# Three score tiles to one exp, half-length DFTs and a planned order of matmuls in an attention-plus-spectral-filter kernel

## The chip, the cores and the metric

The kernel runs on one core of a Trainium2 chip. The metric is the device time of one execution in microseconds. A run is called fast or slow here as the records label it: slow is a run more than 1.5% above the fastest of the same kernel. Times are medians of all runs of a session with the range beside them; ratios are of fast runs only: the mean time of one kernel's fast runs over the mean of the other's fast runs of the same rounds, so not quite the ratio of the medians that are quoted. Engines in the profile: PE is TensorE's matmuls, PEld its weight loads, DVE is VectorE, ACT is ScalarE, POOL is GpSimd, SP the queue that issues most transfers.

## The reference, cut to what matters

```python
def reference(A_x, A_wqkv, A_wo, B_x, B_w_r, B_w_i):     # S = 2048, D = 448, H = 16, Dh = 28, bf16
    # A: full softmax attention
    q, k, v = split(A_x @ A_wqkv)
    p = softmax(einsum("bhqd,bhkd->bhqk", q, k) * Dh ** -0.5)
    a = einsum("bhqk,bhkd->bhqd", p, v).reshape(B, S, D) @ A_wo
    # B: a filter in the frequency domain
    X = rfft2(B_x.astype(float32)) * (B_w_r + 1j * B_w_i)
    b = irfft2(X, s=(S, D)).astype(bfloat16)
    return concatenate([a, b], axis=-1)                  # ... (cut)
```

The exp of 16 x 2048 x 2048 scores is ScalarE's. With four heads side by side in 32-row strips of TensorE (the kernel's `tile_position`; four such score matmuls take 0.33 us until the next group starts, in the trace of the kernel before), there are 1024 score tiles of 128x512. Everything else (projections, both DFTs, output projection) has to find room on the other engines beside those exps.

## The kernel before

An exp takes two score tiles (1024 columns). The scores of four tiles are issued ahead of it, the value matmuls and one step of other work behind it, and two matmuls of zeros per round:

```python
while n < NU:                                   # NU = 512 pairs of tiles
    for m in pair: emit_act(m)                  # ACTIVATE Exp, 128x1024
    for m in reversed(pair): emit_st(m + NST)   # score matmuls, 28 rows of a 32-row strip each
    for m in pair: emit_pv(m)                   # value matmuls, 32 columns each
    ...                                         # (cut) one step of a projection or of the DFT
    if kc_l < KC - 1:
        emit_dummy(dbg.get("dummies", 2))       # matmuls of zeros, 128x128x512, into the accumulator
```

The softmax sums are brought to a 128x16 tile before the reciprocal:

```python
for t in range(4):
    ins = e.matmul(zv[:, 4*t:4*t+4], oaug[:, g, 128*t:128*(t+1)], identb[:, 128:132], start=True, stop=True)
...
e.reciprocal(rzT[:, g, :], zv)                  # 128x16
...                                             # (cut) spread by one copy and 16 small matmuls
```

The DFT of length 2048 is done as 128 x 16, with twiddle products on VectorE and 16-row matmuls on TensorE.

The softmax here doesn't subtract the row's maximum and nothing guards it: scores larger than these inputs give would overflow.

Of the kernel before, what the change touches and what calls it, by code (L numbers as in the profile page):

```python
# [12 lines left out]
_ENG = ("sp", "act", "pe", "dve", "pool")  # L13


class Prog:

    def __init__(self, nc, sems):
        self.nc = nc
        self.streams = {e: [] for e in _ENG}  # L20
        self.sems = sems
        self.count = {name: 0 for name in sems}
        self.wm = {e: {name: 0 for name in sems} for e in _ENG}
        self.trk = {}
        self.consts = set()
        self.csem = {"sp": "dma_sp", "act": "act", "pe": "pe", "dve": "dve", "pool": "pool"}
        self.ninstr = {e: 0 for e in _ENG}
        self.dma_sems = set(n for n in sems if n.startswith("dma") or n.startswith("out"))
# [8 lines left out]
    def _need_waits(self, eng, reads, writes):  # L37
# [14 lines left out]
        for k in reads:  # L52
            en = self._entry(k)
            add(en["w"])
# [5 lines left out]
        return waits  # L60

    def _emit_waits(self, eng, waits):
        for s, v in sorted(waits.items()):
            semh = self.sems[s]
            self.streams[eng].append(lambda e, semh=semh, v=v: e.wait_ge(semh, v))
            self.wm[eng][s] = v
            self.ninstr[eng] += 1

    def op(self, eng, fn, reads=(), writes=(), sem=None, inc=1, signal=True):
        waits = self._need_waits(eng, reads, writes)  # L70
        self._emit_waits(eng, waits)
        if sem is None:
            sem = self.csem[eng]
        if signal:
            self.count[sem] += inc
            ev = (sem, self.count[sem])
            semh = self.sems[sem]
            self.streams[eng].append(lambda e, fn=fn, semh=semh, inc=inc: fn(e).then_inc(semh, inc))
        else:
            ev = None  # L80
            self.streams[eng].append(lambda e, fn=fn: fn(e))
        self.ninstr[eng] += 1
        for k in reads:
            if k in self.consts:
                continue
            en = self._entry(k)
            if ev is not None:
                en["r"].append(ev)
        for k in writes:
            en = self._entry(k)  # L90
            if ev is not None:
                en["w"] = ev
                en["r"] = []
        return ev

    def dma(self, eng, fn, reads=(), writes=(), sem=None):
        if sem is None:
            sem = {"sp": "dma_sp", "pool": "dma_pool", "act": "dma_act"}[eng]
        assert sem in self.dma_sems
        return self.op(eng, fn, reads=reads, writes=writes, sem=sem, inc=16)  # L100
# [19 lines left out]
def _lowprec(nc, msg, thunk):  # L120
    with nc.allow_low_precision(msg):
        return thunk()




def partb_constants():
    S, D = 2048, 448
    KD = 225
    NQ = 4  # L130
    NBQ = [15, 14, 14, 14]
    KD0 = [0, 60, 116, 172]
    d = np.arange(D)
    kd = np.arange(KD)
    CD = np.zeros((128, 4, 450), np.float64)
    ang = 2 * np.pi * np.outer(np.arange(D), kd) / D
    full = np.concatenate([np.cos(ang), -np.sin(ang)], axis=1)
    full[:, 225] = 0.0
    full[:, 225 + 224] = 0.0
    for c in range(3):  # L140
        CD[:, c, :] = full[128 * c:128 * c + 128, :]
    CD[64:128, 3, :] = full[384:448, :]
    s1 = np.arange(128)
    th = 2 * np.pi * np.outer(s1, s1) / 128
    F128 = np.stack([np.cos(th), np.sin(th), -np.sin(th)], axis=1)
    k2 = np.arange(16)
    s2 = np.arange(16)
    W16 = np.exp(-2j * np.pi * np.outer(k2, s2) / 16)
    Cw = W16.real
    Sw = -W16.imag  # L150
    G16 = np.exp(2j * np.pi * np.outer(s2, k2) / 16)
    Gc = G16.real
    Gs = G16.imag
    mats = [Cw.T, Sw.T, -Sw.T, Gc.T, Gs.T, -Gs.T]
    W16C = np.zeros((128, 6, 32), np.float64)
    for i, m in enumerate(mats):
        for r in range(4):
            W16C[32 * r:32 * r + 16, i, 0:16] = m
    th2 = 2 * np.pi * np.outer(np.arange(128), np.arange(16)) / 2048
    TW = np.zeros((128, 16, 4), np.float32)  # L160
    TW[:, :, 0] = np.cos(th2)
    TW[:, :, 1] = -np.sin(th2)
    TW[:, :, 2] = np.sin(th2)
    cfac = np.full(KD, 2.0)
    cfac[0] = 1.0
    cfac[224] = 1.0
    ang2 = 2 * np.pi * np.outer(kd, d) / D
    CRe = cfac[:, None] * np.cos(ang2) / (S * D)
    CIm = -cfac[:, None] * np.sin(ang2) / (S * D)
    CDinv = np.zeros((128, 4, 448), np.float64)  # L170
    quarters = []
    for q in range(NQ):
        k0 = KD0[q]
        nk = 4 * NBQ[q]
        re_hi = min(k0 + nk, 225)
        nre = re_hi - k0
        im_lo = max(k0, 1)
        im_hi = min(k0 + nk, 224)
        nim = im_hi - im_lo
        CDinv[0:nre, q, :] = CRe[k0:re_hi, :]  # L180
        CDinv[64:64 + nim, q, :] = CIm[im_lo:im_hi, :]
        quarters.append(dict(q=q, k0=k0, nb=NBQ[q], nk=nk, nre=nre, nim=nim, imkk0=im_lo - k0))
    return dict(CD=CD, F128=F128, W16C=W16C, TW=TW, CDinv=CDinv, quarters=quarters)

def build_kernel(nc, A_x, A_wqkv, A_wo, B_x, B_w_r, B_w_i, out, do_a=True, do_b=True, defer=24, dbg=None):
    dbg = dbg or {}
    S = 2048
    D = 448
    DH = 28
    NG = 4  # L190
    KC = 16
    QC = 4
    RE = 4
    NST = 3
    scale = float(DH) ** -0.5

    sem_names = ["pe", "act", "dve", "pool", "dma_sp", "dma_pool", "dma_act", "dma_xa", "dma_xb", "dma_bw", "dma_wqk", "dma_wv", "dma_wo", "dma_cst", "out0", "out1", "out2"]
    ctx = ExitStack()
    with ctx:
        sems = {n: ctx.enter_context(nc.semaphore("s_" + n)) for n in sem_names}  # L200
        P = Prog(nc, sems)

        bf16np = mybir.dt.np(BF16)
        cst_np = np.zeros((128, 256), dtype=np.float32)
        cst_np[:, 0:128] = np.eye(128, dtype=np.float32)
        for j in range(4):
            cst_np[32 * j, 128 + j] = 1.0
        cst_h = nc.inline_tensor(cst_np.astype(bf16np), name="cst_bf16")
# [3 lines left out]
        xAT = sb("xAT", [128, 4, S])  # L212
        wq = sb("wq", [128, 4, NG, 128])
        wk = sb("wk", [128, 4, NG, 128])
        wv = sb("wv", [128, 4, 512])
        wo = sb("wo", [128, NG, 448])
        qT = sb("qT", [128, NG, S])
        kT = sb("kT", [128, NG, S])
        Vaug = sb("Vaug", [128, KC, 512])
        ET = sb("ET", [128, RE, 1024])  # L220
        oaug = sb("oaug", [128, NG, 512])
        onrm = sb("onrm", [128, NG, 512])
        rzT = sb("rzT", [128, NG, 16])
        rzrep = sb("rzrep", [128, 4, 128])
        identb = sb("identb", [128, 256])
        zmm = sb("zmm", [128, 512])
        astg = sb("astg", [128, 3, 448])
        bzero = sb("bzero", [128, 448]) if not (do_a and do_b) else None

        PS_all = ctx.enter_context(nc.psum_tensor("PS_all", [128, 4096], F32))  # L230
        ST_ps = PS_all[:, 0:NST * 1024]
        ACC_ps = PS_all[:, 3072:3584]
        MISC_ps = PS_all[:, 3584:4096]

        xa = A_x[0]
        col0 = [0, 128, 256, 320]
        for c in range(4):
            P.dma("sp", lambda e, c=c: e.dma_start_transpose(xAT[:, c, :], xa[:, col0[c]:col0[c] + 128]),  # L238
                  writes=[("xAT", c)], sem="dma_xa")
            P.consts.add(("xAT", c))  # L240

        WQK = [("wq", c) for c in range(4)]
        WKK = [("wk", c) for c in range(4)]
        WVK = [("wv", c) for c in range(4)]
        WOK = [("wo", g, j) for g in range(NG) for j in range(4)]
        P.op("dve", lambda e: e.memset(wq[:], 0.0), writes=WQK)
        P.op("dve", lambda e: e.memset(wk[:], 0.0), writes=WKK)
        P.op("pool", lambda e: e.memset(wv[:], 0.0), writes=WVK)
        P.op("pool", lambda e: e.memset(wo[:], 0.0), writes=WOK)
        P.op("pool", lambda e: e.memset(zmm[:], 0.0), writes=["zmm"])  # L250
        P.dma("pool", lambda e: e.dma_start(identb[:, :], cst_h.ap()[:, :]), writes=["identb"], sem="dma_cst")

        wrows = [(0, 128, 0), (0, 128, 128), (0, 128, 256), (64, 128, 384)]
        wst_holder = []

        def setup_weights():
# [734 lines left out]
```

## Time and profile before

| what | value | how to read it |
|---|---|---|
| time | 695.67 us (694.11 to 696.61, 3 runs) | |
| span of the profiled run | 691.8 us | all shares of the page are of this |
| first exp, end of the last | 28.0, about 663.4 us | 28 us before and 28 us after the exps |
| ScalarE busy with exps | 482.5 us | 153 us of idle time between them |
| zeros on TensorE | 480 matmuls, 164.7 us busy | work that computes nothing |

One more line of the page of the kernel before: the clock that was granted to TensorE in 40 slices of the span, in tenths of full speed.

```profile
PEclk9879999996999996889989967897985889965659
```

It is at full speed for most of the run, with half-clock slices near the end.

### The profile page before, as it was taken

What the parts mean: (1) busy time and instruction counts of PE and PEld (TensorE: products, weight loads), DVE (VectorE), ACT (ScalarE), POOL (GpSimd) and SP (SyncE); (2) the same over time, 40 slices, a digit from 0 to 9 for tenths busy, and PEclk for the clock granted to TensorE, in tenths of its full rate; (3) what the DMA queues carried; (4) which work ended last, traced back from release to release, by engine and by line L of the source; (5) the groups of instructions that cost most, each with busy time, mean ns of one, the idle gap of its engine ahead of it and who ended that gap; (6) DMA issues with size and microseconds to landing.
All of it is one profiled execution on the core that took longest, in us unless ns stands there. A gap on an engine that the chain in (4) does not pass through costs nothing.

```text
span 691.8 us, 11149 instructions
## 1 busy us (share of the span) xinstructions
PE 548.5 (79%) x4614; PEld 173.3 (25%) x4614; DVE 356.2 (51%) x718; ACT 483.8 (70%) x513; POOL 48.3 (7%) x38
## 2 busy tenths in 40 slices
PE   0598899967997975688797685997858868989677
PEld 0122233322321222222122222321222223212223
DVE  1323333375336368853735659336484473542856
ACT  0156698974997984679988755997874769976510
POOL 7710000000030000003000000120000000000000
PEclk9879999996999996889989967897985889965659
DMA  9900000000000200000000200000000200000003
GB/s 226 204 1 0 1 1 1 1 1 0 2 1 8 48 1 1 1 1 1 1 1 21 34 1 1 1 1 1 1 1 1 54 1 1 1 1 1 1 7 127
DMA packets 39138, 13.17 MB, mean 19 GB/s; under 512 B 34112, under 2 KB 38464, under 8 KB 39088
## 3 DMA queue, kind: packets, MB, share of 16 engines
q1 hardware_dynamic: 38272, 10.92, 7.2%
q0 software_dynamic: 816, 1.55, 0.7%
q8 instruction: 36, 0.59, 0.3%
q14 instruction: 14, 0.11, 0.1%
HBM read 4.60 MB, written 3.67 MB: 12 GB/s over the span
## 4 chain that ended last, share of the span: by engine, by line
PE 42%; DVE 31%; ACT 12%; issue 9%; DMA 3%; SPq 2%; POOL 1%; DVEq 0%; ACTq 0%; POOLq 0%
ACT ET L810 12%; PE PS_all L846 9%; PE PS_all L798 7%; PE PS_all L831 6%; PE PS_all L342 5%; DVE BT L690 5%; DVE Y1T L736 3%; PE PS_all L538 3%; DVE Y1T L733 3%; DVE Atr L596 2%; PE PS_all L359 2%; PE PS_all L642 2%; PE PS_all L470 2%; DVE Atr L595 2%; SPq L238 1%
## 5 line engine op out<-in xcount | busy, mean ns | idle before, releaser
L810 ACT ACTIVATE ET<-PS_all 128x1024 bf16<-128x1024 f32 x512 | 482.5, 1070 | 178.8 <-PE PS_all L798 175.6
L846 PE MATMUL PS_all<-zmm 128*128 128x512 bf16 x480 | 164.7, 429 | 0.0
L798 PE MATMUL PS_all<-qT,kT 28*128 28x512 bf16 x1024 | 112.1, 427 | 24.7 <-ACT ET L810 18.5
L831 PE MATMUL PS_all<-ET,Vaug 128*32 128x512 bf16 x1024 | 112.8, 430 | 0.0
L798 PEld LDWEIGHTS PS_all<-qT,kT 28*128 28x128 bf16 x1024 | 26.3, 92 | 155.5 <-ACT ET L810 112.7
L831 PEld LDWEIGHTS PS_all<-ET,Vaug 128*32 128x32 bf16 x1024 | 26.6, 94 | 72.6 <-issue 71.3
L342 PE MATMUL PS_all<-xAT,wq 128*128 128x512 bf16 x64 | 22.7, 461 | 27.2 <-DVE wq L268 18.8
L846 PEld LDWEIGHTS PS_all<-zmm 128*128 128x128 bf16 x480 | 31.8, 101 | 49.1 <-issue 45.3
L690 DVE COPY BT<-PS_all 128x512 bf16<-128x512 bf16 (+2 forms) x16 | 35.0, 2186 | 15.2 <-PE PS_all L687 15.2
L555 POOL MEMSET Atr<- 128x3840 bf16 x4 | 13.2, 3303 | 397.7 <-PE PS_all L614 397.7
L647 DVE CAST AT<-PS_all 128x512 bf16<-128x512 f32 (+2 forms) x32 | 20.2, 632 | 39.9 <-PE PS_all L642 39.9
L647 DVE CAST Xq<-PS_all 128x512 bf16<-128x512 f32 (+2 forms) x32 | 20.3, 633 | 35.8 <-PE PS_all L642 35.8
L726 PE MATMUL PS_all<-F128sb,BT 128*56 128x128 bf16 (+2 forms) x64 | 13.7, 290 | 23.7 <-DVE Y1T L736 17.0
L642 PE MATMUL PS_all<-Xq,W16sb 16*32 16x512 bf16 (+2 forms) x256 | 22.4, 426 | 4.9 <-DVE AT L647 4.9
L733 DVE CAST Y1T<-PS_all 56x128 bf16<-56x128 f32 (+2 forms) x64 | 18.0, 282 | 15.0 <-PE PS_all L729 13.4
L348 DVE CAST qT<-PS_all 128x512 bf16<-128x512 f32 x16 | 11.1, 692 | 27.2 <-PE PS_all L342 27.2
L541 DVE CAST X<-PS_all 128x450 bf16<-128x450 f32 x16 | 10.0, 627 | 29.2 <-PE PS_all L538 29.2
L538 PE MATMUL PS_all<-CD,xBT 128*128 128x450 bf16 x64 | 19.6, 408 | 6.7 <-DMA CDinv<-cst_cdinv 6.0
L348 DVE CAST kT<-PS_all 128x512 bf16<-128x512 f32 x16 | 11.1, 692 | 26.3 <-PE PS_all L342 26.3
L363 DVE CAST Vaug<-PS_all 128x512 bf16<-128x512 f32 x16 | 11.1, 692 | 23.6 <-PE PS_all L359 23.6
L342 PE MATMUL PS_all<-xAT,wk 128*128 128x512 bf16 x64 | 20.0, 413 | 3.2 <-DVE AstF L577 1.9
L470 PE MATMUL PS_all<-wo,onrm 128*128 128x448 bf16 x64 | 18.0, 423 | 5.6 <-DVE AstF L577 2.6
(90 smaller groups left out, 601.7 us busy)
## 6 DMA issues: line engine op xcount, KB each, us to landing
out_dram<-astg SPq DMA_DIRECT2D x32, 112.0 KB, 1.7
Y1T<-in_A_wqkv_dram SPq DMA_DIRECT2D x3, 336.0 KB, 4.3
CD<-cst_cd POOLq DMA_DIRECT2D x1, 450.0 KB, 4.2
CDinv<-cst_cdinv POOLq DMA_DIRECT2D x1, 448.0 KB, 4.4
Wsb<-in_B_w_r_dram SPq DMA_DIRECT2D x2, 224.0 KB, 4.0
Wsb<-in_B_w_i_dram SPq DMA_DIRECT2D x2, 224.0 KB, 3.4
wo<-in_A_wo_dram POOLq DMA_DIRECT2D x16, 24.5 KB, 4.0
Wsb<-in_B_w_r_dram SPq DMA_DIRECT2D x1, 240.0 KB, 4.1
```

The lines of the kernel that those rows point to most:

```text
L342: ins = e.matmul(mv, wsb[rlo:rhi, c, g, :], xAT[rlo:rhi, c, 512 * n:512 * (n + 1)], start=(c == 0), stop=(c == 3))
L348: P.op("dve", lambda e: e.tensor_copy(dst[:, g, 512 * n:512 * (n + 1)], mv), reads=[mkey], writes=[key])
L470: ins = e.matmul(mv, onrm[:, g, 128 * tl:128 * (tl + 1)], wo[:, g, :], start=(g == 0), stop=(g == NG - 1))
L538: ins = e.matmul(mv, xBT[rlo:rhi, c, s2::16], CD[rlo:rhi, c, :], start=(c == 0), stop=(c == 3))
L642: ins = e.matmul(o, W16sb[32 * r:32 * r + 16, wi, :], rhs, start=(term == 0), stop=(term == 1), tile_position=(32 * r, 32 * r))
L647: P.op("dve", lambda e, pout=pout, b=b, nbg=nbg: e.tensor_copy(dst[:, pout, b:b + nbg, :], MISC_ps[:, 0:nbg * 128].rearrange("p (b k) -> p ...
L690: P.op("dve", lambda e, pp=pp, b0=b0, nbat=nbat: e.tensor_copy(BT[:, pp, :, 4 * b0:4 * b0 + 4 * nbat].rearrange("p s k -> p k s"), MISC_bf ...
L733: P.op("dve", lambda e, si=si, s2b=s2b: e.tensor_copy(Y1T[0:nre, q, s2b, :], MISC_ps[0:nre, si * 128:si * 128 + 128]), reads=["MISC"], wri ...
L798: ins = e.matmul(stv[:, jj * 512:(jj + 1) * 512], kT[32 * j:32 * j + KH, g, 128 * kc:128 * (kc + 1)], qT[32 * j:32 * j + KH, g, 512 * qc:5 ...
L810: P.op("act", lambda e: e.activation(ET[:, etslot, :], stv, ACT.Exp, scale=scale), reads=[("ST", stslot)], writes=[("ET", etslot)])
L831: ins = e.matmul(ACC_ps[32 * j:32 * (j + 1), :], Vaug[:, kc, 32 * h:32 * (h + 1)], ET[:, etslot, jj * 512:(jj + 1) * 512], start=False, st ...
L846: ins = e.matmul(ACC_ps, zmm[:, 0:128], zmm[:, 0:512], start=False, stop=False)
```

## The change

The intent: three tiles to one exp (fewer instructions; exps in a row start 0.919 us apart at 1024 elements), a DFT that halves its length once and then multiplies directly by cosine and sine matrices (no twiddles, dense matmuls), and an order of matmuls planned by a list scheduler that knows a cost for each instruction. The zeros are gone. The diff is a new kernel; its core, cut:

```diff
-            P.op("act", lambda e: e.activation(ET[:, etslot, :], stv, ACT.Exp, scale=scale), ...)   # 128x1024
+    TU = 3
+            P.op("act", lambda e: e.activation(ET[:, t % NE, 0:n], PS[:, b0:b0 + n], ACT.Exp, scale=scale),
+                 reads=[("ST", t % 2)], writes=[("ET", t % NE)], cost=0.833e-3 * n + 0.08)          # 128x1536
-                    emit_dummy(dbg.get("dummies", 2))
+        KEEP = 0
-                P.op("dve", ... e.reciprocal(rzT[:, g, :], zv) ...)                                 # 128x16
+                P.op("dve", lambda e: e.reciprocal(rs[:, i, :], MISC), reads=["MISC"], writes=[("rs", i)], cost=0.68)
+                                                                                                    # 128x512
+            if cur[0] is not None and now + mm_cost(cur[0].kreads) <= st_at + 0.35:
+                step_job()            # one matmul of other work, if the plan says that it fits before the next scores
+                continue
... (cut: DFT stages as dense matmuls, complex products on GpSimd, weights loaded on ScalarE's queue)
```

`MISC` is the one PSUM bank that all other work shares: projections, DFT stages, softmax sums and output projections go through it one after the other. Six banks hold scores, one the value accumulator.

## The prediction

> **What bounds the kernel now.** I read the page's busy shares first, then the groups of instructions, then busy time by stretch, then the timeline. The page's first part and the two lines that matter of its groups:
>
> ```profile
> PE 548.5 (79%) x4614; PEld 173.3 (25%) x4614; DVE 356.2 (51%) x718; ACT 483.8 (70%) x513; POOL 48.3 (7%) x38
> ...
> L810 ACT ACTIVATE ET<-PS_all 128x1024 bf16<-128x1024 f32 x512 | 482.5, 1070 | 178.8 <-PE PS_all L798 175.6
> L846 PE MATMUL PS_all<-zmm 128*128 128x512 bf16 x480 | 164.7, 429 | 0.0
> ```
>
> No engine is saturated. The exp on ACT is the one large piece that nothing can avoid: 482.5 us busy, and 175.6 us of its idle time ended with a score matmul (L798). The tile's own listing puts the first exp at 28.0 us and the last at 662.4, about 663.4 with its own length. So the span of 691.8 is 28 us of prologue, 635 us with exps (482.5 busy, about 153 idle) and 28 us of tail. The first two are what a new kernel can win.
>
> Why are the scores late? Busy time by stretch (span; PE, PEld, DVE, ACT, POOL busy with counts; granted clock; DMA) shows two regimes:
>
> ```profile
> 190.25:207.54 17.29, 15.81 (x181) 4.18 (x177) 6.68 (x11) 17.29 (x20) 5.91 (x2) 1.00 0.00 1
> ...
> 259.43:276.72 17.29, 10.24 (x95) 3.89 (x95) 14.30 (x40) 8.36 (x9) 0.00 (x0) 0.61 0.00 1
> ...
> 622.62:639.92 17.30, 16.35 (x107) 3.83 (x106) 5.17 (x6) 11.76 (x13) 0.00 (x0) 0.57 0.00 1
> ```
>
> In the first, the clock is full and ACT is never idle. In the second, VectorE is the busy one (twiddle products and the strided copy L690, 2.43 us at its largest); the in-order PE stands behind the single MISC bank and the scores stand behind it. In the third, PE is busy but at half clock and needs about 3 us for a round of two exps. So the present bound changes: the DFT's VectorE chain, then a PE slowed by its clock, then ACT.
>
> The pace of ACT alone comes from the timeline (start, length, engine, group):
>
> ```profile
> 191.71 16.65 ACT L810 ACTIVATE ET<-PS_all 128x1024 bf16<-128x1024 f32 x18
> ...
> 305.38 0.39 PE L798 MATMUL PS_all<-qT,kT 28*128 28x512 bf16 x4
> ...
> 305.71 0.40 PE L831 MATMUL PS_all<-ET,Vaug 128*32 128x512 bf16 x4
> ...
> 306.50 0.59 PE L846 MATMUL PS_all<-zmm 128*128 128x512 bf16 x2
> ```
>
> Eighteen exps in 16.65 us, the last one 1.03 long: (16.65 - 1.03)/17 = 0.919 us from start to start. Four score matmuls in different row strips take 0.33 us until the next group starts, four value matmuls as well.
>
> [...] 617 to 634 us is solid PE work at 0.50, with much of it in 16-row matmuls. [...] The trace: RECIPROCAL of 16 elements takes 258 ns, where casts out of PSUM of 450 and 512 elements (627 and 692 ns) extrapolate to about 175 ns for 16. [...]
>
> **The change part by part.**
>
> Exp: 512 of 1024 elements become 341 of 1536 and one of 512. [...] 341 x 1.346 + 0.5 = 459 us, against 512 x 0.919 = 471. The larger instruction is worth only 12 us; the gain must come from the 153 us of idle.
>
> PE: the 480 dummies go, also the 16-row DFTs, twiddle transposes and packing transposes. From the order of the new program I counted 1024 score matmuls in 342 groups, 256 groups of four value matmuls, and 328 bursts of other work holding 388,640 columns. Cost at full clock: groups 342 x 0.33 = 113 and 256 x 0.33 = 84; [...] Sum 395 us, or 1.155 us per exp of 1.346. PE is 86% used and no longer the bound, if it stays warm; cold it would need about twice that, 2.1 us per exp. Nearly all new DFT matmuls use 112 to 128 rows and columns, so I expect warm stretches without dummies.
>
> VectorE: about 130 evacuations of 0.63 to 0.69 us, some 90 us, come in place of 356. The complex products go to POOL: eight sets of seven instructions of 512 elements[...]. In the program order they have over 100 exps (130 us) before the last is needed: hidden.
>
> The one addition I distrust is RECIPROCAL. Before it ran on 128x16; now on 128x512, sixteen times, reading the only MISC bank. If the surplus over a cast is per element, (258 - 158)/16 = 6.2 ns, so 158 + 512 x 6.2 = 3.3 us[...]. The scheduler that fixed the order gave it 0.68. Until it ends no other matmul group may use the bank, and the PE queue is in order. In 12 of the 15 cases before the tail just one score group comes between this step and the next MISC user. From the normalizing matmul at t: reciprocal ends near t+3.75, PE goes on at t+3.9, does some 0.5 us of the burst and 0.45 of scores, so ACT gets work at t+4.85. ACT has work left for two exps, 2.69 us, from an end of exp at about t+0.4: idle 1.75 us. Three cases have two score groups and lose about 0.4. Sum 12 x 1.75 + 3 x 0.4 = 22 us.
>
> The 2.9 us holes also make some clock windows fall: in the 3.4 us stretches of the kernel before, stretches with less than about 1.8 us of PE time are mostly followed by 0.50. If 60% of 15 holes do that and each costs one window and a half at 2.1 instead of 1.346 us per exp, about 1.7 us, that is 15 us.
>
> Prologue: only one input is transposed on the way in, and the weights load through the ACT queue beside it. Before, weights landed at 17.7 us after the queue's transposes; I put the first scores at 22.5 and the first exp at 23 (was 28). PE starts cold: 4 us. Five places where the order has a whole projection squeezed in ahead of the scores: 5 us.
>
> Tail, from the last exp: values and evacuation 1.4, normalizing matmul 0.6, reciprocal 3.3, product 0.8, four output groups in one bank at cold clock (1.5 matmul + 1.0 evacuation and waits each) 10, last store 2.2, waits 0.6: 19 us (was 28).
>
> Sum: 23 + 459 + 22 + 15 + 9 + 19 = 547 us of span; measured time was 3.9 above the span, so 551. I take a little less, 542, since the reciprocal may be quick (then 22 and 15 vanish and 2.5 of the tail: about 512).
>
> **The rivals.** (a) The reciprocal is cheap[...]: 512. One small sample speaks for neither[...]. (b) The clock falls without dummies: at a third of the exps cold, 114 x 0.8 = 90 us more, about 620. For it: value and score groups alone fill only 0.58 of 1.346 us. Against: the order spreads other work over nearly all exps (0.45 to 0.6 us each, 0.25 in the weight-transposing stage), which is 70 to 90% busy. (c) POOL is slower than assumed or waits on VectorE[...]. (d) DMA: about 8 MB of constants and inputs before the DFT; at the 226 GB/s of the first slice it takes 40 us, and the transforms come later in the order. Hidden.
>
> **Range and chances.** Low end: fast reciprocal, 512 plus a little, 515. High end: [...]more cold stretches, 575. Even rival (b) is far below 682, so faster is near sure: 0.98, with 0.01 for each other outcome.
>
> **What would show it.** Right: ACT busy near 460 us, exps 1.34 us start to start in runs; RECIPROCAL at 3 to 4.5 us with the following PE matmul waiting for it, and ACT idle of 1 to 2 us sixteen times; clock at 1.00 in most slices with dips near those; first exp near 23; tail near 19. Wrong: RECIPROCAL under 1 us; clock at 0.5 over long stretches; PE waiting on POOL or DMA; ACT idle spread evenly over all exps, which would mean that PE, not ACT, sets the pace.

The pace of 1.346 us, and with it the 459, was an estimate; measured afterwards it is right (0.919 us for 1024 elements and 1.346 for 1536 make 0.834 ns per element and 65 ns fixed). TensorE's 395 us were 113 + 84 + 162 for columns + 36 for changes of shape. (In e7, below, 14 matmuls of zeros occupy TensorE for 3.12 us at full clock, 2.3 columns per ns, by which the 388,640 columns take 169 us.) That the products are hidden was an assumption, and a longer estimate of the reciprocal stood behind the upper ends of 575 and 4.5 us. What the prediction says of stretches of 3.4 us, the traces bear out: in both, every recorded stretch of one clock but the last is a whole multiple of 3.41 us. Cut into such stretches, from 26.52 us on, the trace of the kernel before has 26 with less than 1.8 us of TensorE's work, and all 26 are followed by one at 0.50; of the other 168, 31 are. In the changed kernel it is 17 of 17 and 42 of 145.

## The result, and the profile after

The changed kernel took 648.07 us (median of 4, 636.28 to 658.25) against 696.14 us (694.11 to 699.39) of the kernel before in the same session; the ratio of fast runs is 0.9189, with a 95% interval of 0.9121 to 0.9257. It is faster, and 103 us slower than the range's middle of 545, 73 above its upper end. Its scatter of 3.4% is new, too: the kernel before stays within 0.8%.

Lines of the changed kernel's page, of the same kinds as those shown of the kernel before:

```profile
PE 505.3 (80%) x3095; PEld 159.3 (25%) x3128; DVE 169.3 (27%) x197; ACT 472.3 (74%) x343; POOL 104.9 (17%) x106
...
PEclk9999856769697979797975779697975879969895
...
L611 ACT ACTIVATE ET<-PS 128x1536 bf16<-128x1536 f32 x342 | 471.0, 1475 | 140.9 <-PE PS L601 140.2
...
L640 DVE RECIPROCAL rs<-PS 128x512 f32<-128x512 f32 x16 | 53.7, 3358 | 9.0 <-PE PS L622 4.2
```

VectorE went from 356 to 169 us and is no bound any more. ScalarE still waits 140 us for scores (L601), and the clock has a comb of dips. The timeline of the changed kernel around one of the sixteen reciprocals shows where a dip begins (start, length, engine, group, idle time before it):

```profile
220.71 0.39 PE L601 MATMUL PS<-qT,kT 28*128 28x512 bf16 x3 [0.62 <-ACT ET L611]
220.72 3.36 DVE L640 RECIPROCAL rs<-PS 128x512 f32<-128x512 f32 x1 [0.55 <-PE PS L601]
...
224.13 1.53 PE L414 MATMUL PS<-FR,R 128*112 128x512 bf16 x3 [2.70 <-DVE rs L640]
225.59 0.61 PE L601 MATMUL PS<-qT,kT 28*128 28x512 bf16 x3
...
226.31 1.45 ACT L611 ACTIVATE ET<-PS 128x1536 bf16<-128x1536 f32 x1 [2.96 <-PE PS L601]
```

TensorE's order has a DFT matmul (L414) next, which needs the bank that the reciprocal reads, so it stands still for 2.70 us. When it goes on, a score group takes 0.61 us where it took 0.39: half clock (0.50 in the record, third row below). From now on **the length of a score group of three is my clock gauge**: 0.39 us at full and 0.61 us at half speed. It is needed because the clock record is not to be had for the start: busy time by stretch of the changed kernel (span; PE, PEld, DVE, ACT, POOL busy; clock; DMA share, GB/s) says 1.00 at 45 us, where every score group of the timeline takes 0.61 us.

```profile
45.00:48.41 3.41, 3.41 (x23) 1.07 (x22) 0.69 (x1) 2.25 (x3) 0.00 (x0) 1.00 0.15 29
221.88:225.30 3.42, 1.17 (x3) 0.48 (x3) 2.20 (x1) 1.46 (x2) 1.14 (x1) 0.72 0.00 0
225.30:228.70 3.40, 3.40 (x15) 1.01 (x14) 0.00 (x0) 1.45 (x1) 0.01 (x1) 0.50 0.00 0
300.34:303.76 3.42, 3.24 (x27) 1.34 (x26) 0.47 (x1) 3.42 (x3) 0.00 (x0) 1.00 0.00 0
```

The last row is the state that the prediction took as the rule: clock 1.00, ScalarE busy all the time. The third is the state after a hole: TensorE busy in every microsecond at half clock, ScalarE at 1.45 of 3.40. Of the 329 score groups of three that the trace resolves, 92 are at half clock, 39 of them before 150 us.

Adding up the 634.5 us of the profiled run: 29.9 before the first exp, 471.0 of exps, 17.8 after the last. The remaining 116 us are idle time between exps: 36.6 in front of the first exp after 15 reciprocals (2.44 each), 6.8 in one wait for rows of the filter weights near 100 us, 15.0 in four projections that the plan had put off until they stood in a row ahead of the scores (4.16, 3.84, 3.43, 3.56), and **57 us in short gaps, 47 of them next to score groups at half clock**. The prediction had 22 us for the first of these and 24 us for all the rest.

### The profile page after: what moved, and what is told of

It is laid out like the page before. It is cut to its first block, busy times and chain, and to the rows that moved or that the text cites. A ratio compares the mean times of both kernels' runs of the same rounds, so it can differ in the third digit from the quotient of the medians.

```text
span 634.5 us, 7421 instructions
## 1 busy us (share of the span) xinstructions
PE 505.3 (80%) x3095; PEld 159.3 (25%) x3128; DVE 169.3 (27%) x197; ACT 472.3 (74%) x343; POOL 104.9 (17%) x106
## 4 chain that ended last, share of the span: by engine, by line
PE 64%; DVE 16%; ACT 9%; issue 5%; DMA 4%; SPq 2%; ACTq 0%; DVEq 0%
PE PS L601 14%; PE PS L622 12%; ACT ET L611 9%; DVE rs L640 7%; PE PS L437 7%; PE PS L414 6%; PE PS L363 5%; PE PS L379 5%; PE PS L504 5%; PE PS L536 4%; PE PS L653 3%; SPq L253 2%; DMA Wst<-in_B_w_i_dram 1%; DVE qT L368 1%; DMA xAT<-in_A_x_dram 1%
## 5 line engine op out<-in xcount | busy, mean ns | idle before, releaser
L611 ACT ACTIVATE ET<-PS 128x1536 bf16<-128x1536 f32 x342 | 471.0, 1475 | 140.9 <-PE PS L601 140.2
L601 PE MATMUL PS<-qT,kT 28*128 28x512 bf16 x1024 | 154.5, 448 | 24.8 <-ACT ET L611 12.9
L622 PE MATMUL PS<-ET,Vaug 128*32 128x512 bf16 x1024 | 117.4, 449 | 1.8 <-ACT ET L611 0.8
L601 PEld LDWEIGHTS PS<-qT,kT 28*128 28x128 bf16 x1024 | 33.8, 93 | 137.5 <-ACT ET L611 66.1
L640 DVE RECIPROCAL rs<-PS 128x512 f32<-128x512 f32 x16 | 53.7, 3358 | 9.0 <-PE PS L622 4.2
L437 PE MATMUL PS<-R,T 112*113 112x512 bf16 (+1 forms) x128 | 48.6, 486 | 9.5 <-DVE rs L640 7.2
L363 PE MATMUL PS<-xAT,wk 128*128 128x512 bf16 (+1 forms) x55 | 22.9, 492 | 35.6 <-DMA xAT<-in_A_x_dram 23.7
L414 PE MATMUL PS<-FR,R 128*112 128x512 bf16 x128 | 44.5, 454 | 7.6 <-DVE rs L640 2.7
L504 PE MATMUL PS<-T,R 113*128 113x448 bf16 (+1 forms) x128 | 39.2, 417 | 7.4 <-DVE rs L640 5.9
L536 PE MATMUL PS<-R,FR 128*128 128x448 bf16 x128 | 35.2, 396 | 7.0 <-DVE rs L640 5.2
L379 PE MATMUL PS<-wst,xAT 128*128 128x112 bf16 (+1 forms) x256 | 36.5, 260 | 3.6 <-DVE rs L640 2.4
```

The source lines that it names most:

```text
L363: mms.append(lambda e, c=c, rlo=rlo, rhi=rhi: e.matmul(MISC, wsb[rlo:rhi, c, g, :], xAT[rlo:rhi, c, 512 * n:512 * (n + 1)], start=(c == 0) ...
L379: mms.append(lambda e, c=c, rlo=rlo, rhi=rhi, kq=kq: e.matmul(MISC[:, 112 * kq:112 * kq + 112], xAT[rlo:rhi, c, 128 * (4 * n + kq):128 * ( ...
L414: mms.append(lambda e, c=c: e.matmul(MISC[0:112, :], src[:, c, 112 * b:112 * b + 112], F1v[:, i, c, :], start=(c == 0), stop=(c == 7)))
L437: mms.append(lambda e, ti=ti, part=part, v=v, q=q: e.matmul(MISC[0:kn, :], T1[0:112, v, q, k0:k0 + kn], Sd[0:112, q, part, 512 * h:512 * h ...
L504: mms.append(lambda e, ti=ti, sg=sg, p=p, v=v, b=b, kn=kn: e.matmul(MISC[:, 0:448], X[0:kn, b, sg, p, ks], T2[0:kn, v, b, :], start=(ti == ...
L536: mms.append(lambda e, r=r, tt=tt, n=n: e.matmul(MISC[:, 0:448], F2v[:, a % 4, r, tt, :], Y[:, tt, r, :], start=(n == 0), stop=(n == 7)))
```

## The experiments

Two theories were set against each other first. **H**: the holes behind the reciprocal make the clock fall, and the cold spells that follow cost more than the holes. **D**: the clock falls anyway, as no zeros feed TensorE; the reciprocal costs its own holes alone. The table gives the runs with three tiles to an exp (the others are told below); "half" is the number of score groups of three at half clock among those resolved in the profiled run (323 to 335 of 342), a single look. The profiles of e2, e12 and e14 are of runs labelled slow.

| run | median us (range, 4 runs) | half | last exp ends, us |
|---|---|---|---|
| changed kernel | 648.1 (636.3 to 658.3) | 92 | 617 |
| e1 copies for reciprocals (wrong result) | 562.8 (560.8 to 567.0) | 62 | 548 |
| e2 holes filled with zeros | 601.0 (589.4 to 601.7) | 47 | 584 |
| e3 compact reciprocal | 583.0 (576.1 to 600.8) | 69 | 562 |
| e4 warm start | 641.6 (638.9 to 643.0) | 104 | 619 |
| e5 true cost in the plan | 657.5 (652.5 to 666.1) | 127 | 623 |
| e6 = e3, other order of jobs | 590.2 (587.1 to 597.3) | 78 | 545 |
| e7 = e6 and two bursts of zeros | 591.8 (569.2 to 609.1) | 46 | 533 |
| e9 = e5, slack filled | 606.1 (605.0 to 606.3) | 17 | 576 |
| e10 = e6, slack filled | 559.6 (557.9 to 561.0) | 2 | 517 |
| e13 = e10, zeros of one row | 646.9 (635.9 to 671.7) | 70 (by single matmuls, see e13) | 592 |
| e16 = e3, slack filled | 567.6 (565.1 to 570.0) | 16 | 550 |
| **e11 = e10, short tail, weights later** | **537.4 (535.0 to 540.1)** | 5 | 516 |

The kernel before had medians of 695.8 to 698.7 us in these sessions.

### What the reciprocals cost (e1, e2, e3)

e1 keeps the order of every engine and makes the sixteen instructions short:

```diff
-                P.op("dve", lambda e: e.reciprocal(rs[:, i, :], MISC), ...
+                P.op("dve", lambda e: e.tensor_copy(rs[:, i, :], MISC), ...
```

> The changed kernel with the 16 RECIPROCALs of 128x512 (3.36 us each) replaced by copies of the same tile (about 0.5 us); order on every engine is the same; the result is wrong on purpose. Theory H (the holes make the clock fall, and the cold spells after them cost more than the holes): the 15 holes go (-37 us) and with them most of the cold spells (-40 to -55 us): about 550 to 560 us, granted clock in the profile above 0.93. Theory D (the clock falls anyway, because no dummies keep TensorE fed; the reciprocal costs its hole alone): about 600 us, granted clock still near 0.83 to 0.87.

It took 562.8 us, ratio 0.8088 (0.8037 to 0.8139) against 0.9189 of the changed kernel. Two lines of its page:

```profile
PEclk9999999999999999999999999998997889889995
...
L611 ACT ACTIVATE ET<-PS 128x1536 bf16<-128x1536 f32 x342 | 465.4, 1562 | 77.4 <-PE PS L601 77.0
```

The comb of dips is gone, and 72 us of the profiled span with it. Half of that, 37 us, were the holes themselves. D falls; H holds in its direction, though the spells cost about as much as the holes, not more. But 53 of e1's 62 half-clock groups lie before 150 us: a cold start that the reciprocal has nothing to do with, and that the clock line (all 9) does not show.

e2 keeps the reciprocals and their holes on ScalarE and has TensorE multiply zeros meanwhile:

```diff
+            if hole[0]:                     # first matmul in the shared bank behind a softmax sum
+                hole[0] = False
+                fill_hole(12)               # 12 matmuls of zeros, 128x128x512, into the accumulator
```

> The changed kernel with the reciprocals kept, and 12 matmuls of zeros (128x512, 0.22 us each at full clock, 2.6 us in all) put on TensorE where it otherwise stands idle behind a reciprocal. Theory H: the holes of ScalarE stay at 2.4 us, but the clock does not fall after them, so the cold spells go: 580 to 595 us, granted clock above 0.93. Theory D: the clock goes on falling elsewhere, within 10 us of the changed kernel, about 630 to 640 us.

589 us in its fast run and 600 to 602 in the three others, one of which was profiled: waits of about 2.1 us on ScalarE stayed behind most reciprocals, and 40 to 50 us went with the cold spells. The timeline of e2 shows in addition what ends a cold spell, here one that had lasted since the start:

```profile
76.31 0.61 PE L603 MATMUL PS<-qT,kT 28*128 28x512 bf16 x3 [0.52 <-issue]
76.84 0.62 PE L624 MATMUL PS<-ET,Vaug 128*32 128x512 bf16 x4
77.39 4.16 PE L678 MATMUL PS<-zmm 128*128 128x512 bf16 x12
...
81.54 0.39 PE L603 MATMUL PS<-qT,kT 28*128 28x512 bf16 x3
```

Four microseconds of nothing but full-array matmuls, and the next score group takes 0.39 us.

e3 is correct: it takes the sums to a 128x16 tile as the kernel before did, so the reciprocal is short again.

```diff
-            [lambda e: e.matmul(MISC, cid[:, 2, :], oaug[:, i, :], start=True, stop=True)]
+            for t in range(4):
+                zmms.append(lambda e, t=t: e.matmul(MISC[:, 4*t:4*t+4], oaug[:, i, 128*t:128*t+128], cid[:, 2, 0:128:32], ...))
+            ... e.reciprocal(rz[:, i, :], MISC[:, 0:16]) ...   # then one copy, 16 broadcast matmuls, one product on VectorE
```

> A correct version: the sums of the 512 queries are taken to a 128x16 tile by 4 small matmuls, 16 reciprocals each partition (0.26 us in the kernel before), spread by one copy and 16 matmuls of 32 columns, as the kernel before did; all on TensorE and VectorE between two exps of the ring. Theory H: near the run with copies, 555 to 570 us, granted clock above 0.9. Theory D: about 600 to 610 us.

576 to 601 us, median 583: most of the gain, its median 13 us above the range I gave it, with 69 groups still at half clock and a wide scatter.

### Is it standing still, or too little work? (e5, e4, e7, e8)

The scheduler had planned with 0.68 us for an instruction of 3.36. e5 corrects that one number:

```diff
-  e.reciprocal(rs[:, i, :], MISC), reads=["MISC"], writes=[("rs", i)], cost=0.68)
+  e.reciprocal(rs[:, i, :], MISC), reads=["MISC"], writes=[("rs", i)], cost=3.4)
```

> The changed kernel with one number of its scheduler's table put right: the 128x512 RECIPROCAL is entered as 3.4 us instead of 0.68 us. Nothing is computed differently; TensorE's list now puts score and value matmuls behind the sum instead of a matmul that must wait for the bank the reciprocal reads. If the holes are the scheduler's error: the 15 waits of 2.4 us on ScalarE go (-37 us), and where the clock is lost by a TensorE that stands still, most of the cold spells too: 580 to 600 us. If a TensorE that is only half fed for 3.4 us loses the clock as well, the holes go and the cold spells stay: about 600 to 615 us.

Neither expectation was right: 657.5 us, slower than the changed kernel, with 127 groups at half clock. Of the 16 us by which its profiled run is longer, 10 lie in a longer tail (27.9 against 17.8 us) and 6 before it. Its timeline at one reciprocal is the most instructive:

```profile
267.05 11.12 ACT L611 ACTIVATE ET<-PS 128x1536 bf16<-128x1536 f32 x8
...
272.10 3.36 DVE L640 RECIPROCAL rs<-PS 128x512 f32<-128x512 f32 x1 [0.55 <-PE PS L622]
272.84 0.39 PE L601 MATMUL PS<-qT,kT 28*128 28x512 bf16 x3 [0.53 <-ACT ET L611]
...
273.16 0.40 PE L622 MATMUL PS<-ET,Vaug 128*32 128x512 bf16 x4
...
274.19 0.39 PE L601 MATMUL PS<-qT,kT 28*128 28x512 bf16 x3 [0.62 <-ACT ET L611]
...
275.53 0.61 PE L601 MATMUL PS<-qT,kT 28*128 28x512 bf16 x3 [0.62 <-ACT ET L611]
```

There is no hole: ScalarE runs eight exps on end across the reciprocal, as the plan intended. But in those 3.4 us TensorE has only scores and values, which keep it busy for 1.66 us. At 275.5 the clock is gone, and but for moments the score groups stay at 0.61 us until 380 us. So the clock is lost **not where ScalarE waits but where TensorE lacks work**, and H has to be put that way. The changed kernel's own trace had said so twice: after the reciprocals at 73.2 and 253.5 us a score group already takes 0.61 us, before TensorE stands still for the bank.

e4 puts 80 matmuls of zeros at the very start:

```diff
+            for _ in range(80):
+                ins = e.matmul(MISC, zmm[:, 0:128], zmm[:, :], start=True, stop=True)
```

> The changed kernel with 80 matmuls of zeros on TensorE during the 24 us in which it waits for the transposed input. In the changed kernel the three score matmuls of an exp start 0.54 us apart (half clock) from 30 to about 63 us. If that cold start is one that ends only because of load, the warm start takes the first 33 us from 2.0 to 1.35 us per exp: 8 to 12 us less, about 628 us; the rest of the run is not changed, neither theory of the holes is touched. If the clock is lost anyway by the first wait, no change within the noise of 1.7%.

No change: 641.6 us. Busy time by stretch of e4 shows why (the transposed input arrives at 22.9 us):

```profile
16.00:20.00 4.00, 4.00 (x20) 1.67 (x17) 0.18 (x2) 0.00 (x0) 2.16 (x4) 1.00 1.14 237
20.00:23.40 3.40, 0.59 (x4) 0.21 (x3) 0.00 (x0) 0.00 (x0) 0.00 (x0) 1.00 1.10 253
23.40:26.80 3.40, 2.62 (x7) 0.47 (x5) 0.69 (x1) 0.00 (x0) 0.00 (x0) 0.70 1.10 386
26.80:30.20 3.40, 2.61 (x19) 1.02 (x18) 0.69 (x1) 1.91 (x2) 2.74 (x3) 0.50 1.07 408
```

TensorE was warm (20 matmuls in 4.00 us), was busy for 0.59 us of the next 3.40, and was at half clock (0.50) before the first exp; it stayed there to about 140 us.

e8 is the kernel before without its zeros:

```diff
-                    emit_dummy(dbg.get("dummies", 2))
+                    emit_dummy(dbg.get("dummies", 0))
```

> The kernel before without its 480 matmuls of zeros (a correct kernel). If dummies are what holds the clock in such a kernel: the granted clock falls from 0.86 to 0.7 or less and the time rises, to 720 to 780 us. If they only take TensorE's time: faster, 640 to 680 us, at about the same clock.

685.4 us (680.7 to 692.0), ratio 0.9804 (0.9736 to 0.9872): the clock fell from about 0.86 to 0.67, as D's reading of the zeros says, and yet it was not slower, which neither expectation had. The record calls the verdict unclear at its mark of 2%; the interval lies below 1. There the zeros cost at least as much as the clock that they bought.

e6 moves two due times of e3's plan, and e7 adds two bursts of 14 zeros:

```diff
-        for q in range(4): w_job(q, ...)            # filter transposes
-        ...                                         # first DFT stage
+        for q in range(2): w_job(q, ...)
+        ...                                         # first DFT stage
+        for q in range(2, 4): w_job(q, ...)
-   slot_time(...) - (7 if g == 0 else 20)
+   slot_time(...) - lead,  lead = 7, 20, 20, 70     # projections of the last head group 50 us earlier
+   if t in (6, 12): burst(14)                       # e7 only
```

> The version with the compact reciprocal, and two due times moved: the filter transposes of the odd columns behind the first DFT stage, and the projections of the last head group 50 us earlier. No work is added or taken away. Expected: the 6.6 us wait on the filter's rows near 99 us goes, and the waits of 2.5 to 7.5 us on ScalarE after 430 us, where projections stand in a row ahead of a score matmul (about 15 us): 555 to 568 us against 576 to 585 of that version. If the clock decides and not these waits: within its scatter, 575 to 600 us.

> As the run before, and 14 matmuls of zeros (128x512, 4.2 us at half clock) at two places of the first stage, before the 7th and the 13th exp. In the runs with copies and with the compact reciprocal the score matmuls stay 0.61 us long (half clock) from 30 to 130 us. If a dense burst ends the cold start and nothing then loses the clock: 50 exps take 1.35 instead of 2.0 us, less the two bursts: -22 to -28 us against the run before, 530 to 545 us. If the clock is lost again at once: the bursts cost 6 to 8 us and it is slower than the run before.

e6 missed: 590.2 us. The waits did go (two over 1.6 us are left, both about 3 us) and the last exp ended at 545 instead of 562 us, but the tail after it grew from 18 to 40 us: output projections that had run beside the exps now stood in line for the one shared bank, 2.5 us each. e7 gave 569 and 575 us in two runs and 609 in the other two. In the profiled one the first burst brought the clock at once (4.58 us for the 13 zeros that the trace has of it, where 4.2 were expected, and 0.39 for the score group behind it; the second burst, at full clock, took 3.12 us until the next scores), and it was lost in the second of these stretches, where TensorE had 128-column filter transposes of 0.43 us to do and little else:

```profile
60.30:63.70 3.40, 3.31 (x24) 0.89 (x22) 0.69 (x1) 3.40 (x4) 0.00 (x0) 1.00 0.39 159
63.70:67.10 3.40, 2.35 (x24) 0.98 (x24) 1.54 (x3) 3.40 (x4) 0.00 (x0) 1.00 0.00 0
67.10:70.50 3.40, 3.09 (x20) 1.26 (x20) 1.23 (x2) 3.40 (x3) 0.00 (x0) 0.51 0.00 0
```

### Filling the slack, and what about the filling counts (e9, e10, e16, e13)

The scheduler knows where its plan leaves TensorE without work. There, and only there, the next four kernels multiply zeros:

```diff
             nxt = [x for x in nxt if x > now]
+            nd = int((min(nxt) - now) / 0.22)       # whole 128x128x512 matmuls that fit into the planned idle time
+            if nd > 0 and stptr[0] < NT:
+                fill(min(nd, 16))
             P.free["pe"] = min(nxt) + 0.01
```

> The run with the reciprocal's true cost, and in every stretch of 0.22 us or more in which the scheduler's own plan leaves TensorE without work, as many matmuls of zeros (128x512, 369 in all) as fit. The reciprocals, their 3.36 us and the order of the real work stay. If the clock is lost where TensorE lacks dense work (not where ScalarE waits, and not through the reciprocal itself): the cold spells go, 657 us becomes 565 to 595 us, granted clock above 0.93. If the zeros only take time from a TensorE that is busy anyway: 650 to 690 us.

> The run with the jobs put in another order, filled in the same way (331 zeros). That run had 590 us, the last exp ended at 545 us, half clock from 30 to 90, 230 to 285 and in places near 315. If missing dense work is what loses the clock: no stretch of half clock longer than 10 us after the first, last exp at 510 to 520 us, and with its tail of 40 us 550 to 562 us. If not: 585 us or more.

> The version with the compact reciprocal (583 us), its slack filled with zeros as in e9 and e10, without the other order of jobs. With the clock held, what remains against the filled other order (560 us) is the wait on the filter's rows (6.6 us) and the waits of projections after 430 us (15 to 20 us), against a tail shorter by 20 us: 555 to 568 us. If the other order was needed to hold the clock: over 575 us.

e9: 606.1 us against 657.5 without the filling, with the reciprocals and the order of the real work as they were; less gain than I expected, as the projections in a row (up to 7 us each) and short cold stretches behind them (near 430, 453 and 480 us) remained. e10: 559.6 against 590.2. e16: 567.6 against 583.0, so the filling alone holds the clock well in the order the change's own scheduler made, and the other order adds 8 us on top. The scatter falls with it: under 0.6% in e9 and e10. Two lines of e10's page:

```profile
PEclk9999999999999999999999999989999999999855
...
L619 ACT ACTIVATE ET<-PS 128x1536 bf16<-128x1536 f32 x342 | 468.4, 1492 | 44.0 <-PE PS L609 42.0
```

25.3 of these 44.0 us of idle time are the wait for the first scores. Between the exps, 19 us are left of 116.

e13 is e10 with one row in each of its 331 zeros:

```diff
-                    ins = e.matmul(ACC, zmm[:, 0:128], zmm[:, :], start=shut, stop=shut)
+                    ins = e.matmul(ACC, zmm[0:1, 0:128], zmm[0:1, :], start=shut, stop=shut)
```

> The filled version with the long tail (560 us), with every matmul of zeros reading one row instead of 128 (1x512, same number, same places, same duration by the row of dummies; nothing else differs). If the time in which TensorE is occupied holds the clock: 558 to 562 us again, clock 0.97. If what counts is how much of the array works: the zeros no longer hold it, half clock from 30 to 90 us, and in the places of the unfilled order, 590 to 640 us.

646.9 us against 559.6: all of the gain is lost. Of the 1024 score matmuls, 239 ran at half clock (about 0.6 us each where others take 0.39); it was 243 in e6, which has no zeros, and 14 in e10. Busy time by stretch of e13, and below it of e10 at the same time:

```profile
222.00:225.40 3.40, 3.40 (x23) 1.14 (x21) 0.73 (x2) 3.40 (x4) 0.00 (x0) 1.00 0.00 0
225.40:228.80 3.40, 3.40 (x45) 1.38 (x45) 1.51 (x4) 3.40 (x4) 0.00 (x0) 1.00 0.00 0
228.80:232.20 3.40, 3.40 (x26) 1.06 (x22) 1.38 (x2) 3.40 (x4) 0.00 (x0) 0.67 0.02 5
232.20:235.60 3.40, 3.40 (x10) 1.28 (x10) 0.00 (x0) 2.20 (x2) 0.00 (x0) 0.50 0.00 0
```

```profile
225.40:228.80 3.40, 3.40 (x28) 1.50 (x26) 0.69 (x1) 3.40 (x4) 3.24 (x4) 1.00 0.00 0
228.80:232.20 3.40, 3.32 (x25) 1.27 (x24) 0.42 (x1) 3.40 (x4) 0.86 (x2) 1.00 0.00 0
```

In e13 TensorE is busy in every one of 10.2 us, and the clock goes all the same. **Busy time is not what holds the clock; zeros of 128 rows hold it and zeros of one row do not.** That the share of the array in use is what counts is the plainest reading, but it is not shown: columns were not varied, and what scores and values count for is open, as three or four of them run side by side in the strips (0.33 us to the next group for either), and in e5 TensorE was idle for half of the time too. How much such work is enough these runs do not tell either.

The time of e13 is not the clock's alone. It is 57 us slower than e6, with as much half clock. The one-row zeros run into the scores: 60 of the 331 start within 0.03 us of a score matmul, and in 41 groups the third score starts over 0.1 us late, in 40 of them behind a zero. (So the length of a group is no clock gauge in e13, and single matmuls were used for the table.) How the 57 us divide is open; the evidence on the clock is the count and the stretches above.

### Three tiles or two (e12, e14, e15)

The undone part, on top of e11 (below): two tiles to an exp, a ring of three pairs.

```diff
-    TU = 3
-    NE = 5
+    TU = 2
+    NE = 7
-        SLOT = 1.37
+        SLOT = 0.93
```

> The filled version with the short tail, with two score tiles to one exp instead of three (512 exps, a ring of three pairs, seven ET tiles; the scheduler plans with the shorter slot and fills its own slack). If ScalarE sets the pace now: the pitch of 0.919 us of the kernel before against 1.344 us, 470.5 us of exps against 459.7 us, so 10 to 14 us slower than that version, 547 to 552 us. If TensorE or the scheduler's order sets it: within 5 us of it, or faster, as the ring of three pairs gives more room.

864 us (849 to 864, of which only the 849 is labelled fast). Neither expectation was near. TensorE is busy for 95% of the span; the timeline in the middle of it:

```profile
250.66 0.61 PE L611 MATMUL PS<-qT,kT 28*128 28x512 bf16 x2
251.20 0.62 PE L632 MATMUL PS<-ET,Vaug 128*32 128x512 bf16 x4
...
251.75 1.10 PE L419 MATMUL PS<-FR,R 128*112 128x512 bf16 x2
```

A group of two scores takes the same 0.54 us to the next matmul as a group of three does at half clock (and 0.32 at full clock, in e15, as a group of three does in the changed kernel): the third score takes no time of its own. So 512 groups instead of 342 cost an estimated 170 x 0.33 = 56 us more of TensorE at full clock, and 170 x 0.54 = 92 us at half. This kernel starts cold and is bound by TensorE at half clock, and its score groups are 0.61 us long from the start to 780 us, but for some 16 us after 472. (The clock record, 1.00 up to its first change near 485 us, had misled me into "its first 500 us" in the next expectation.) Two bursts of zeros near its start (e14), or one before every 32nd exp (e15):

```diff
+                    if t in (9, 18):                 # e14;   e15: if t % 32 == 9 or t == 18
+                        fill(14)
```

> The two-tile version that ran at half clock for its first 500 us (864 us), with 14 dense matmuls of zeros before its 10th and 19th exp. If that kernel was merely caught in the cold state it started in, and its mix of work can hold the clock but not regain it: about 550 to 570 us. If its mix cannot hold the clock either: a good part of the run is cold again, over 620 us.

> The same with a burst of 14 dense zeros before every 32nd exp (17 bursts, 3 us each at full clock, some 45 us at most). No cold spell can last longer than 32 exps: 560 to 610 us, and 46 us more than the three-tile version at the most from the bursts, so the three tiles are worth 10 to 14 us there by the pitch of the undisturbed exps (0.919 against 1.344 us).

e14: 736 us in one run, 873 to 891 in three, with one and the same program. The profiled one, a slow one, has the clock after its first burst at 38 us, loses it at 63 us, and has it again for some 9 us before 569 and from 798 us on. In that run its mix of matmuls does not hold the clock; the fast run was not profiled. e15: 660.8 us (660.3 to 664.0), clock 0.93. That is 123 us above e11, of which the 17 bursts are about 51 (3.0 us each in its timeline); the rest I have not divided between the 56 us of score groups and the cold stretches that remained. The expectation's 10 to 14 us was the wrong sum: it counted ScalarE alone.

### The version that beats both (e11)

e10 with two small parts more:

```diff
+        tail_banks = [[MISC, "MISC"], [PS[:, 0:512], ("ST", 0)], [PS[:, 1536:2048], ("ST", 1)]]
+            if jb.i == 1 and jb.bk is not None and stptr[0] >= NT:       # no scores are left to issue
+                jb.bk[:] = min(tail_banks, key=lambda b: P.ready("pe", (), [b[1]]))
-            P.dma("act", ... e.dma_start(wst[rlo:rhi, c, :], A_wqkv[...])   # beside the transposes of the input
+            P.dma("sp", ...)                                                # behind them
```

> As the run before, and two small parts: after the last score matmul the output projections and the last inverse DFTs take turns in three banks (their own and two of the free score banks) instead of waiting 0.8 us each for the evacuation of one; and the weights are loaded behind the transposed input, as in the kernel before, not beside it. Expected: first exp at 22 to 24 us instead of 29 (-5 to -7 us), the tail 20 to 24 us instead of 40 (-16 to -20 us): 525 to 540 us.

537.4 us (535.0 to 540.1), correct, ratio 0.7693 (0.7655 to 0.7732) to the kernel before. The tail is 17 us instead of 41. The first exp starts at 26.5 us, later than the 22 to 24 I expected but 3.7 before e10's: the four transposes are issued in 9.75 us, where the changed kernel took 17.98, once no weights load beside them, and now the copies of the weights end last.

```profile
PE 493.0 (92%) x3708; PEld 177.7 (33%) x3767; DVE 136.8 (26%) x228; ACT 470.6 (88%) x343; POOL 88.6 (17%) x92
...
PEclk9999999999999999999999999997999999999999
...
L621 ACT ACTIVATE ET<-PS 128x1536 bf16<-128x1536 f32 x342 | 469.3, 1493 | 44.6 <-PE PS L611 42.4
```

ScalarE is busy for 88% of the span, and 24 of its 44.6 us of idle time lie before the first exp: it is the bound now, as the prediction had wanted it.

## Why the prediction was wrong

The direction was right and the time was not: 648 us against a range that ended at 575. Its sum for the span was 547 us, the profiled span 634.5. Of the 87.5 us between them the short gaps, put down to the clock, have 38, the holes 15, busy exps 12, squeezed projections 10, the prologue 7 and a transfer 7; the tail gives back 1.

- **Pace of the exps: right.** 1.346 us start to start was predicted; twenty-one exps from 296.02 us take 28.37 us, the last 1.46 long, which gives 1.346. The busy sum is 471.0 instead of 459 because an exp that waits takes its full 1.45 us.
- **Length of the reciprocal: right.** 3.3 us predicted, 3.358 measured; with 0.258 for 128x16 in the kernel before that makes 6.25 ns per element.
- **Holes: too small.** 22 us predicted, 36.6 measured. The account took the first matmuls after the hole at full clock; the timeline has them at half (1.53 us for three, where three of another DFT step take 0.86 at full clock near 249 us). And it had three short holes of 0.4 us; the shortest of the fifteen was 1.71.
- **The step that failed: the clock.** "If 60% of 15 holes do that and each costs one window and a half [...] that is 15 us", with "PE starts cold: 4 us", stood on "Nearly all new DFT matmuls use 112 to 128 rows and columns, so I expect warm stretches without dummies". Measured: 57 us in short gaps where the account had 19, and 92 half-clock score groups. Both factors were too small. A half-clock group follows each of the 15 reciprocals within 6 us, not 60% of them. In eight cases first and last half-clock group lie at most 5 us apart, as assumed; in the other seven it is 8 to 33 us. And the cold start lasted 16 groups, to 61 us, in place of some six (4 us at about 0.7 us each). At half clock TensorE needs 2.04 us a round (14 exps from 29.92 to 58.48 us; 2.16 in the 13 from 326.75 us on; 2.1 was estimated), is then nearly always busy (9.72 of 10.23 us from 45 us on), and often does not come back. e2's burst of zeros shows one thing that ends a spell; what else does stays open, for with the same order of work the first one ended at 61 us in the changed kernel and at 139 in e1. e1 shows it by taking the reciprocals away, e9, e10 and e16 by filling what TensorE lacks, and e13 by taking the rows out of that filling.
- **Rival (b) was put aside by the wrong measure.** The prediction argued against it that TensorE would be "70 to 90% busy". e13 shows 100% busy and a lost clock. The prediction had the hint in hand: its own third stretch of the kernel before, solid work at half clock (17.00 of 17.00 us busy, clock 0.50), "much of it in 16-row matmuls". It read the hint as a property of 16-row DFTs. In amount the rival came close: 297 of the 1024 score matmuls ran at half clock, where it had a third of the exps.
- **Prologue: 7 us too small.** 23 predicted, 29.9 measured: the four transposes took 17.98 us to issue with the weights loading beside them, and 9.75 with the weights behind them in e11.
- **Rival (d), transfers, nearly right:** one wait of 6.8 us for rows of the filter weights. **Rival (c), GpSimd, right:** 1.15 to 1.27 us a product, never waited for.
- **Squeezed projections:** 5 predicted, 15.0 measured, in four places.
- **Tail: right.** 19 predicted, 17.8 measured.
- **Three tiles: "worth only 12 us"** counted ScalarE alone. On TensorE the third tile's scores take no time of their own (0.54 us for two or three at half clock), an estimated 56 us by e12's timeline. How that compares with the other parts is not shown: no run undoes the new DFT alone, whose effect is seen only in VectorE's busy time (356 to 169 us) and in the time of the whole.
- **Slips in the sums.** Twice 1.155 is 2.3 us, not 2.1; 8 MB at 226 GB/s take 35 us, not 40; and the 3.9 us between span and time compare two executions: 1.8 is the difference in every run listed with its span. None changes the outcome.

With its holes and cold spells taken away the change does what the sum had hoped for: e10 lies at 560 us, and e11, with two further parts, at 537.

## What to carry to other kernels

Here TensorE kept its clock with zeros of 128 rows in its slack (e10: 14 of 1024 score matmuls at half clock) and lost it with zeros of one row (e13: 239), so look at what TensorE is given in each short stretch, and read the clock off the length of a repeated matmul group (0.39 or 0.61 us here), not off the busy share (10.2 of 10.2 us in e13). A static plan is only as good as its table: put measured durations in, and then look at what the plan does to the other engines, for a plan without waits can be slower than one with them (e5, 657.5 us against 648.1). Where a plan leaves TensorE idle, filling just that idle time with zeros of 128 rows was cheap here and made the time repeatable (e10, 559.6 us, within 0.6%); zeros in addition to a full plan were not (some 51 us in e15).
